# Softmax rows copied to fp32r-typed tiles ahead of three quarters of the last layer's transposes

## The chip, the cores and the metric

One core of a Trainium2 chip runs the whole program. Its engines work side by side, each through its own queue: TensorE (PE, with its weight loads shown apart as PEld), VectorE (DVE), ScalarE (ACT), GpSimd (POOL) and SyncE (SP), which here issues the DMAs. The metric is the device time of one execution, in microseconds; before the change the median of three runs is 1212.86 us (1212.85 to 1212.88).

## The reference

Three layers in sequence, on 8 sequences of 576 positions, in fp32. First an attention over 32 memory slots (8 heads of 64), then a token and channel MLP with residuals, and last the layer that the change touches, four causal attention experts of which each position uses two:

```python
logits = x @ w_gate                      # top 2 of 4 experts, softmax over the two
for e in range(E):                       # E = 4, Hd = 64
    q, k, v = x @ wq[e], x @ wk[e], x @ wv[e]
    scores = scale * (q @ k.transpose(0, 2, 1))
    scores = np.where(causal, -1000000000.0, scores)
    scores = scores - scores.max(-1, keepdims=True)
    a = np.exp(scores)
    a /= a.sum(-1, keepdims=True) + 1e-09
    ye = a @ v @ wo[e]
    out += mask[..., None] * w * ye      # mask: this expert is one of the position's two
```

## The kernel before, in words

Products that need more than fp32r precision are made of three fp32r products: a number is split into a high part of type fp32r and the rest (`split`, `mm3`, L207). The last layer is the last stage of the program, from about 735 us on; the channel MLP's last two chunks of hidden units are computed inside it as filler, in halves of a sequence (`load_2`, `split_2`, `mm1_2`, `load_p2`, `mm2_2`).

**Units.** A unit `n` is one sequence `b` and one expert `e` (n = 4b + e), 32 in all. Its 576 queries are four blocks of 128 rows and a tail of 64; two units (an even and the odd one after it) share one tail of 128 rows. Block `c` sees 128(c + 1) keys, so the blocks have 128, 256, 384 and 512 columns; a unit's four blocks lie side by side in a tile of 1280 columns (`ab`, one of two by the parity of the unit; offsets `aoff`), the tails in `atl`.

**Steps of a unit.** `scores` (L1314 to L1316): the products into PSUM, a masked minimum on VectorE and the exponential on ScalarE into `a`. `norm` (L1344 to L1359): the factors (softmax sum and gate) on VectorE, and then POOL multiplies the four blocks by them, in the order 0, 1, 2, 3 (L1359); the tail is scaled by ScalarE (L1355). `turn` (L1361): TensorE transposes the scaled rows 128x128 at a time into PSUM, as fp32, with an fp32 identity (L1378), and `split` makes high and low parts of them. Block 2 is turned first (3 transposes, and in even units one more of the tail's last columns, L1380), then blocks 0 and 1 together (3), and later block 3 (4) and the tail (`tail_turn`, L1398, 4). `weigh` (L1423) multiplies the transposed rows with the values, and `project` (L1452) makes the output of a sequence from its four experts and stores it.

**The order.** The loop over `t` traces unit `t`'s scores and `norm` and unit `t - 1`'s `turn` and `weigh`, and between them pieces of a list of filler (`some()`). The order in which each engine runs its instructions is then written by the framework, which plays the traced instructions through a simulated timeline (`schedule_with_timeline_sim=True`, with transposes at high priority); the order is fixed in the program, and each engine's queue, SP's too, runs it in order and waits where an operand isn't there.

**Tiles and slots.** A tile name has as many slots as `bufs` says; a new tile of a name waits until all readers of the one that held its slot are done. `u2` (a half's input to the channel MLP, 576 KB) has two slots in the pool `c2`; `p2[1]` borrows one of them. `yb` (a partial sum in `weigh`) has two. The output blocks `osb` have two, from the pool `late` in the last sequence (after `c2` is closed), and there the very last block has two tiles of its own, `oh0` and `oh1`.

Of the kernel before, what the change touches and what calls it, by code (L numbers as in the profile page):

```python
# [9 lines left out]
F32 = mybir.dt.float32  # L10
# [15 lines left out]
def f(ap):  # L26
    return ap.bitcast(F32)
# [140 lines left out]
def fused_kernel(ctx: ExitStack, tc, q, k, v, phi, w_tok1, w_tok2, w_ch1, w_ch2,  # L168
# [695 lines left out]

    c2 = None
    c2_ctx, w3_ctx = ExitStack(), ExitStack()
    u2, uh2, ul2, h2, p2 = {}, {}, {}, {}, {}

    def load_2(j):
        u2[j] = c2.tile([128, KD, SH], F32, name="u2", bufs=2)  # L870
        SP.dma_start(u2[j][:], u_d[:, SH * j:SH * j + SH].rearrange("(c p) s -> p c s", p=128))

    def load_p2(j):
        p2[j] = c2.tile([128, KD, SH], F32, name="u2", bufs=2) if j == 1 else c2.tile([128, KD, SH], F32, name="p2")
        SP.dma_start(p2[j][:], x_d[:, SH * j:SH * j + SH].rearrange("(c p) s -> p c s", p=128))
# [22 lines left out]
    with ExitStack() as sb:  # L898
# [189 lines left out]
        for i in range(NW + LAG):  # L1088
            items = [()] if i == NW else [work[i]] if work[i][0] in WIDE else [(*work[i], 0), (*work[i], 1)]
            for it in items:  # L1090
                if it:
# [10 lines left out]
                    for fc in fcs:  # L1102
# [10 lines left out]
                        if n > WIDE[-1]:  # L1113
                            for _ in range(7):
                                if next(wcl, 0) == 0 and c2 is None:
                                    stg_ctx.close()
                                    c2 = c2_ctx.enter_context(tc.tile_pool(name="c2", bufs=1, side="right"))
                                    load_2(0)
                                    load_2(1)
# [46 lines left out]
    with ExitStack() as sc:  # L1166
# [22 lines left out]
        aoff = [0, 128, 384, 768]  # L1189
        ab = [wk_.tile([128, 1280], F32, name=f"a{i}") for i in range(2)]  # L1190

        atl = wk_.tile([128, 640], F32, name="atl")
# [151 lines left out]
        def norm(n):  # L1344

            b, e = divmod(n, E)
            w = NQ - e % 2
            cf = wk_.tile([128, NQ], F32, name="cf", bufs=2)
            DVE.tensor_scalar_add(cf[:, 0:w], smb[n % 2][:, 0:w], 1e-9)
            DVE.reciprocal(cf[:, 0:w], cf[:, 0:w])  # L1350
            DVE.tensor_mul(cf[:, 0:w], cf[:, 0:w], gt[b][:, e, 0:w])  # L1351
            a = ab[n % 2]
            for c in range(w):
                if c == NQ - 1:
                    ACT.activation(atl[:, 0:S], atl[:, 0:S], AF.Copy, scale=cf[:, c:c + 1])  # L1355
                    continue
                W = 128 * c + 128
                x_ = a[:, aoff[c]:aoff[c] + W]
                POOL.tensor_mul(x_, x_, cf[:, c:c + 1].to_broadcast([128, W]))  # L1359

        def turn(n, c):  # L1361

            e = n % 2
            a = ab[e]
            if n not in aA:
# [10 lines left out]
            with tc.high_priority():  # L1376
                for kc in range(k):
                    PE.transpose(p[:, 128 * kc:128 * kc + 128], a[:, o + 128 * kc:o + 128 * kc + 128], ident[:])  # L1378
                if c == 2 and e == 0:
# [12 lines left out]
        def tail_turn(n):  # L1392
# [3 lines left out]
            with tc.high_priority():  # L1396
                for kc in range(4):
                    PE.transpose(p[:, 128 * kc:128 * kc + 128], atl[:, 128 * kc:128 * kc + 128], ident[:])  # L1398
            split(Bh[:, :, :, 256:320].rearrange("p e k q -> p k e q"), Bl[:, :, :, 256:320].rearrange("p e k q -> p k e q"),
                  p[:].rearrange("p (k e q) -> p k e q", k=4, e=2))  # L1400

        def weigh(n, part):
# [19 lines left out]
            for i, (kc, lo, x) in enumerate(ops):  # L1422
                PE.matmul(p[:, lo:w], lhsT=v_[:, kc, 0, :], rhs=x, start=(i == 0), stop=(i == len(ops) - 1))  # L1423
            t_ = wk_.tile([128, 320], F32, name="yb", bufs=2)
            ACT.activation(t_[0:64, 0:w], p[64:128, 0:w], AF.Copy)
# [26 lines left out]
        def project(b, c):  # L1452
# [3 lines left out]
            cs = slice(0, 128) if last else slice(128 * c, 128 * c + 128)  # L1456
            if b == B - 1 and c == 1:
                for i, w in enumerate((slice(0, 256), slice(256, 512))):
                    p = pp.tile([128, 512], F32, name="g", bufs=GB)[:, 0:256]
                    mm3(p, [((y[0][:, cs], y[1][:, cs]), (woh[:, pr, w], wol[:, pr, w]))  # L1460
                            for pr in range(2) for y in [yT[b, pr][1:]]], late="l")
                    o_ = late.tile([128, 256], F32, name=f"oh{i}")
                    if i:
                        DVE.tensor_copy(o_[:], p)
                    else:
                        ACT.activation(o_[:], p, AF.Copy)
                    SP.dma_start(out[b, cs, w], o_[:])
                return
            p = pp.tile([128, 512], F32, name="g", bufs=GB)
            mm3(p[:], [((y[0][:, cs], y[1][:, cs]), (woh[:, pr, :], wol[:, pr, :]))  # L1470
                       for pr in range(2) for y in [yE[b // 2, pr] if last else yT[b, pr][1:]]], late="l")
            o_ = late.tile([128, 512], F32, name="osb", bufs=2) if late else wk_.tile([128, 512], F32, name="osb", bufs=2)
            if b == B - 1 and c in (3, 0):
# [22 lines left out]
        load_2(2)  # L1496
        load_2(3)
        proj(0, 1, 1, 0, True)
# [4 lines left out]
        for t in range(NE + 2):  # L1503
# [12 lines left out]
            if e == 0:  # L1516
# [6 lines left out]
                if b == B:  # L1523
                    held = [(project, B - 2, c) for c in range(4)]
            elif e == 1:
                if b < B:
                    fill = [(proj, b, 1, i, hf) for i, hf in KQ[2:4]]
                if 0 < b < B - 1 and b - 1 not in HELD:
# [5 lines left out]
            elif e == 2:  # L1534
# [9 lines left out]
                if b + 2 < B:  # L1544
                    fill += [(load_2, 2 * b + 4), (load_2, 2 * b + 5)]
            elif e == 3 and not more:
# [104 lines left out]
```

## Time and profile before

| | |
|---|---|
| median of three runs | 1212.86 us |
| the profiled execution | 1214.76 us |
| its span, first to last instruction | 1213.0 us |
| PE busy | 1165.3 us, 96% |
| PEld busy | 1064.7 us, 88% |
| VectorE busy | 816.3 us, 67% |
| ScalarE busy | 610.8 us, 50% |
| POOL busy | 449.5 us, 37% |
| mean granted clock of TensorE | 0.988 |

The page gives each engine's busy time, the same in 40 equal slices of 30.3 us (a digit is tenths, 9 means 90% or more), the DMA queues, the chain of work that ended last, and groups of equal instructions. The views asked of the trace are a table of busy time by stretches, lists of instructions in order of time, groups by form, the waits and the DMA issues. Matmuls are pipelined: one's duration is longer than the distance to the next.

### The profile page before, as it was taken

The page shows a single profiled execution, that of the slowest core. Times are in us where ns is not written, and L with a number is a line of the kernel's source. Part 1 is how long each engine was busy: PE and PEld are TensorE (multiplying, and loading weights), DVE is VectorE, ACT ScalarE, POOL GpSimd, SP SyncE. Part 2 cuts the span into 40 slices and gives each one's busy share as a digit, 9 for nine tenths or more (in the row PEclk, how much of TensorE's full clock was granted, in tenths as well). Part 3 has the DMA queues.
Part 4 walks back from the last instruction along what each step waited for, and adds up shares of the span by engine and source line. Part 5 has one row for each costly group of instructions (what it writes and reads, how often), then busy time and mean ns, then how long its engine had stood idle before and what let it go on. Part 6 is the DMA issues. An engine that isn't in the chain of part 4 may idle for free.

```text
span 1213.0 us, 23508 instructions
## 1 busy us (share of the span) xinstructions
PE 1165.3 (96%) x8586; PEld 1064.7 (88%) x8586; DVE 816.3 (67%) x1992; ACT 610.8 (50%) x1591; POOL 449.5 (37%) x603
## 2 busy tenths in 40 slices
PE   4899998999999999999999999999999999999998
PEld 3678887999888888889999889999999999999986
DVE  6999998665483756567566514777676767676664
ACT  3565565454442323223322213677676767677775
POOL 2774453442002012112111344545454627383331
PEclk9799999999999999999999999999999999999999
DMA  8896767532370221232123343322333333322522
GB/s 239 251 276 209 215 212 221 171 118 92 97 251 20 105 70 35 71 104 97 43 71 105 96 113 114 88 84 79 84 88 83 102 97 99 94 80 54 166 86 105
DMA packets 133780, 145.07 MB, mean 120 GB/s; under 512 B 35616, under 2 KB 101408, under 8 KB 133664
## 3 DMA queue, kind: packets, MB, share of 16 engines
q1 hardware_dynamic: 133664, 143.57, 39.2%
q8 instruction: 68, 1.11, 0.4%
q14 instruction: 48, 0.39, 0.1%
HBM read 91.10 MB, written 40.89 MB: 109 GB/s over the span
## 4 chain that ended last, share of the span: by engine, by line
PE 79%; DVE 11%; DMA 3%; issue 2%; ACT 2%; POOL 1%; SPq 0%; DVEq 0%; ACTq 0%; POOLq 0%
PE g L207 21%; PE o L207 16%; PE h L207 16%; PE y L1423 4%; PE b L207 3%; PE s L1314 3%; PE b L679 3%; PE t L1378 3%; PE s L1336 1%; DVE ul L670 1%; DVE cy L772 1%; PE g L623 1%; PE g L383 1%; PE g L624 1%; PE g L626 1%
## 5 line engine op out<-in xcount | busy, mean ns | idle before, releaser
L1359 POOL TENSOR_TENSOR a<-a,cf 128x128 f32<-128x128 f32 (+3 forms) x128 | 88.3, 723 | 68.9 <-DVE cf L1351 64.9
L207 PE MATMUL o<-hl,w2h 128*128 128x512 f32 x288 | 112.7, 391 | 0.3 <-DVE hl L931 0.3
L207 PE MATMUL o<-hh,w2l 128*128 128x512 f32 x288 | 112.3, 390 | 0.0
L207 PE MATMUL o<-hh,w2h 128*128 128x512 f32 x288 | 108.7, 392 | 0.2 <-DVE pb L1026 0.2
L930 ACT ACTIVATE hh<-m 128x256 fp32r<-128x256 f32 x96 | 38.9, 416 | 111.8 <-DVE m L1001 72.2
L1303 DVE CUSTOM_DVE_ANT_0 ssb<-s,cmask 128x128 f32<-128x128 f32 (+2 forms) x144 | 68.5, 483 | 27.3 <-PE s L1314 20.5
L1316 ACT ACTIVATE a<-ssb,nb 128x128 f32<-128x128 f32 (+3 forms) x128 | 71.3, 558 | 18.4 <-DVE nb L1303 15.1
L207 PE MATMUL h<-uh,w1h 128*128 128x512 f32 (+2 forms) x200 | 66.5, 334 | 4.7 <-ACT uh L211 4.7
L931 DVE SCALAR_TENSOR_TENSOR hl<-m,hh 128x256 fp32r<-128x256 f32 x96 | 58.2, 615 | 17.6 <-ACT hh L930 15.4
L978 POOL TENSOR_TENSOR tl<-ub,th 128x512 fp32r<-128x512 f32 x12 | 18.1, 1526 | 136.3 <-ACT th L977 136.3
L207 PE MATMUL h<-uh,w1l 128*128 128x512 f32 (+2 forms) x200 | 66.7, 334 | 0.0
L1215 POOL TENSOR_TENSOR xl<-p,xh 128x288 fp32r<-128x288 f32 x60 | 47.4, 811 | 51.8 <-ACT xh L1214 51.6
L207 PE MATMUL h<-ul,w1h 128*128 128x512 f32 (+2 forms) x200 | 66.1, 335 | 0.0
L207 PE MATMUL g<-xh,qkh 128*128 128x288 f32 x232 | 65.3, 301 | 0.0
L207 PEld LDWEIGHTS o<-hh,w2l 128*128 128x128 f32 x288 | 54.1, 188 | 11.3
L207 PE MATMUL g<-xh,qkl 128*128 128x288 f32 x232 | 63.9, 296 | 0.0
L207 PEld LDWEIGHTS o<-hh,w2h 128*128 128x128 f32 x288 | 54.0, 188 | 10.7 <-DVE pb L1026 1.0
L963 POOL TENSOR_TENSOR ub<-ub 128x512 f32<-128x512 f32 x6 | 9.8, 1628 | 144.4 <-DVE ul L214 144.4
L207 PEld LDWEIGHTS o<-hl,w2h 128*128 128x128 f32 x288 | 54.1, 188 | 10.0 <-DVE hl L931 0.6
L214 DVE TENSOR_TENSOR Bl<-t,Bh 128x512 fp32r<-128x512 f32 (+1 forms) x80 | 50.5, 633 | 14.3 <-ACT Bh L211 12.6
L923 DVE SCALAR_TENSOR_TENSOR hl<-h,hh 128x512 fp32r<-128x512 f32 x24 | 16.5, 689 | 59.9 <-ACT hh L922 59.8
L1430 POOL TENSOR_TENSOR yl<-yt,yh 128x256 fp32r<-128x256 f32 x30 | 22.2, 739 | 85.0 <-ACT yh L1429 74.9
(340 smaller groups left out, 4123.8 us busy)
## 6 DMA issues: line engine op xcount, KB each, us to landing
cst<-in_moe_w_ch_dram SPq DMA_DIRECT2D x24, 512.0 KB, 4.8
u_d<-u SPq DMA_DIRECT2D x32, 288.0 KB, 3.6
p_d<-u SPq DMA_DIRECT2D x16, 576.0 KB, 4.2
ub<-u_d SPq DMA_DIRECT2D x9, 1024.0 KB, 5.7
pb<-p_d SPq DMA_DIRECT2D x36, 256.0 KB, 4.1
x_d<-pb SPq DMA_DIRECT2D x36, 256.0 KB, 2.1
u<-u_d SPq DMA_DIRECT2D x16, 576.0 KB, 4.2
p<-x_d SPq DMA_DIRECT2D x15, 576.0 KB, 4.1
```

Of the source, the lines that this page charges most:

```text
L207: PE.matmul(ps, lhsT=a, rhs=b, start=start and i == 0, stop=stop and i == len(seq) - 1)
L214: DVE.tensor_sub(lo, src, f(hi))
L679: PE.matmul(h1[j, fc, "p"][:], lhsT=w[:, kd, :], rhs=x[:, kd, :], start=(part == 0 and i == 0), stop=(part == 1 and i == KD - 1))
L930: ACT.activation(hh, c, AF.Relu)
L931: DVE.scalar_tensor_tensor(hl, c, 0.0, f(hh), op0=OP.max, op1=OP.subtract)
L1215: POOL.tensor_sub(xl[b][:, c, ss], x_, f(xh[b][:, c, ss]))
L1303: DVE.tensor_tensor_reduce(out=out, in0=p, in1=mask, scale=-scale, scalar=least, op0=OP.add, op1=OP.min, accum_out=acc)
L1314: PE.matmul(p[:, 0:W], lhsT=q_[n][:, 128 * c:128 * c + 128], rhs=kk[n][:, 0:W], start=(i == 0), stop=(i == 1))
L1316: ACT.activation(a[:, aoff[c]:aoff[c] + W], s_[:, 0:W], AF.Exp, scale=-1.0, bias=nb[:, 0:1], accum_out=sm[:, c:c + 1])
L1359: POOL.tensor_mul(x_, x_, cf[:, c:c + 1].to_broadcast([128, W]))
L1378: PE.transpose(p[:, 128 * kc:128 * kc + 128], a[:, o + 128 * kc:o + 128 * kc + 128], ident[:])
L1423: PE.matmul(p[:, lo:w], lhsT=v_[:, kc, 0, :], rhs=x, start=(i == 0), stop=(i == len(ops) - 1))
```

## The change

For units 0 to 30, `norm` copies the scaled blocks 0 and 1 (one DMA), the scaled block 3 (another), and for even units the first 512 columns of the scaled tail (a third), as raw bits, from the fp32 tiles to tiles of type fp32r (`ar`, 1280 columns, and `atr`, 512, one slot each). The transposes of these read the copies with an fp32r identity and write PSUM through an fp32r view. Block 2 of every unit, the last unit's blocks, and the tail's last columns are transposed from the fp32 tiles as before. The order of scaling becomes block 2, then 0 and 1, then 3, and the tail's ScalarE product is traced ahead of them.

To make room in SBUF, `u2` gets one slot in `c2` and, for the half j = 1 alone, one in a pool of its own, and the loads of odd halves are traced a unit or more later; `yb` gets one slot; `osb` always comes from the stage's pool, and the last output block takes one of its two slots in place of `oh0` and `oh1`.

```diff
-        u2[j] = c2.tile([128, KD, SH], F32, name="u2", bufs=2)
+        u2[j] = (wk8 if j == 1 else c2).tile([128, KD, SH], F32, name="u2")
...
-        p2[j] = c2.tile([128, KD, SH], F32, name="u2", bufs=2) if j == 1 else c2.tile([128, KD, SH], F32, name="p2")
+        p2[j] = c2.tile([128, KD, SH], F32, name="u2" if j == 1 else "p2")
...
+        identr = wk_.tile([128, 128], F32R, name="identr")
+        ACT.activation(identr[:], ident[:], AF.Copy)
...
-            for c in range(w):
-                if c == NQ - 1:
-                    ACT.activation(atl[:, 0:S], atl[:, 0:S], AF.Copy, scale=cf[:, c:c + 1])
-                    continue
-                W = 128 * c + 128
-                x_ = a[:, aoff[c]:aoff[c] + W]
-                POOL.tensor_mul(x_, x_, cf[:, c:c + 1].to_broadcast([128, W]))
+            copied = n < NE - 1
+            ar[n] = wk_.tile([128, 1280], F32R, name="ar") if copied else a
+            if e % 2 == 0:
+                ar["t"] = wk_.tile([128, 512], F32R, name="atr")
+                ACT.activation(atl[:, 0:S], atl[:, 0:S], AF.Copy, scale=cf[:, NQ - 1:NQ])
+            for cs in ((2,), (0, 1), (3,)):
+                for c in cs:
+                    W = 128 * c + 128
+                    x_ = a[:, aoff[c]:aoff[c] + W]
+                    POOL.tensor_mul(x_, x_, cf[:, c:c + 1].to_broadcast([128, W]))
+                if copied and cs != (2,):
+                    o = slice(aoff[cs[0]], aoff[cs[-1]] + 128 * cs[-1] + 128)
+                    SP.dma_start(f(ar[n][:, o]), a[:, o])
+                if e % 2 == 0 and cs == (2,):
+                    SP.dma_start(f(ar["t"][:, 0:512]), atl[:, 0:512])
...
-            a = ab[e]
+            a, idn, ty = (ar[n], identr, F32R) if n < NE - 1 and c != 2 else (ab[e], ident, F32)
...
-                    PE.transpose(p[:, 128 * kc:128 * kc + 128], a[:, o + 128 * kc:o + 128 * kc + 128], ident[:])
+                    PE.transpose(p[:, 128 * kc:128 * kc + 128].bitcast(ty), a[:, o + 128 * kc:o + 128 * kc + 128], idn[:])
...
-                    PE.transpose(p[:, 128 * kc:128 * kc + 128], atl[:, 128 * kc:128 * kc + 128], ident[:])
+                    PE.transpose(p[:, 128 * kc:128 * kc + 128].bitcast(F32R), ar["t"][:, 128 * kc:128 * kc + 128], identr[:])
...
-            t_ = wk_.tile([128, 320], F32, name="yb", bufs=2)
+            t_ = wk_.tile([128, 320], F32, name="yb")
...
+                o2 = wk_.tile([128, 512], F32, name="osb", bufs=2)
...
-                    o_ = late.tile([128, 256], F32, name=f"oh{i}")
+                    o_ = o2[:, w]
...
-            o_ = late.tile([128, 512], F32, name="osb", bufs=2) if late else wk_.tile([128, 512], F32, name="osb", bufs=2)
+            o_ = wk_.tile([128, 512], F32, name="osb", bufs=2)
...
-        load_2(3)
...
+                if more:
+                    fill += [(load_2, 2 * b + 3)]
...
-                    fill += [(load_2, 2 * b + 4), (load_2, 2 * b + 5)]
+                    fill += [(load_2, 2 * b + 4)]
```

## Rows read from the trace of the kernel before

**Rows 1.** The page, busy shares of the span and busy tenths in 40 slices

```profile
PE 1165.3 (96%) x8586; PEld 1064.7 (88%) x8586; DVE 816.3 (67%) x1992; ACT 610.8 (50%) x1591; POOL 449.5 (37%) x603
...
PE   4899998999999999999999999999999999999998
```

**Rows 2.** Table by stretches of the last layer; the first row names its columns

```profile
core 0: us, PE busy (x) PEld busy (x) DVE busy (x) ACT busy (x) POOL busy (x), PEclk, DMA share, GB/s
776.00:1160.00 384.00, 379.85 (x2840) 370.13 (x2840) 272.62 (x877) 277.45 (x809) 196.69 (x302) 1.00 0.32 89
1160.00:1213.00 53.00, 46.96 (x271) 40.09 (x269) 25.99 (x80) 33.08 (x83) 14.19 (x22) 0.98 0.32 109
```

**Rows 3.** PE's longest wait from 735 us on: total, times, longest

```profile
PE s L1314 <- DMA qa<-qb: 2.1, 1, 2.1
```

**Rows 4.** Products by form: count, busy us, mean ns of one, idle before

```profile
L1378 PE MATMUL t<-ident,a 128*128 128x128 f32 x320 | 48.8, 274 | 0.1
...
L207 PE MATMUL h<-th,sh 128*128 128x256 f32 x144 | 40.7, 282 | 0.0
...
L1398 PE MATMUL t<-ident,atl 128*128 128x128 f32 x64 | 10.0, 275 | 0.2 <-DVE Bt L1390 0.2
...
L1423 PE MATMUL y<-Al,vhl 128*128 128x128 f32 x24 | 5.3, 223 | 0.0
...
L1380 PE MATMUL t<-ident,atl 128*128 128x128 f32 x16 | 4.4, 272 | 0.0
```

**Rows 5.** PE in order of time at 1025 us: start, us, instruction, count

```profile
1025.75 0.82 PE L1378 MATMUL t<-ident,a 128*128 128x128 f32 x6
1026.40 0.27 PE L1380 MATMUL t<-ident,atl 128*128 128x128 f32 x1
```

**Rows 6.** Weight loads of ordinary fp32r products by form, 128 and 64 columns

```profile
L207 PEld LDWEIGHTS g<-vgh,xh 128*128 128x128 f32 x128 | 24.2, 189 | 0.6 <-ACT kk L1235 0.4
...
L207 PEld LDWEIGHTS g<-vgh,xh 128*64 128x64 f32 x32 | 4.3, 134 | 0.0
```

**Rows 7.** Loads of fp32 transposes (L521, L525) and an fp32 product: min/median/max ns

```profile
L525 PEld LDWEIGHTS t<-ident,at x16: 108/110/128, 35.7 to 305.7; 128*64 128x64 f32 x16
...
L521 PEld LDWEIGHTS t<-ident,at x64: 137/141/229, 31.7 to 304.9; 128*128 128x128 f32 x64
...
L393 PEld LDWEIGHTS g<-ones,es x28: 186/190/338, 38.5 to 272.3; 128*128 128x128 f32 x28
```

**Rows 8.** DMA issues: count, KB each, median us from issue to landing

```profile
u<-u_d SPq DMA_DIRECT2D x16, 576.0 KB, 4.2
...
qb<-qa SPq DMA_DIRECT2D x32, 144.0 KB, 2.4
...
y_d<-yl SPq DMA_DIRECT2D x6, 256.0 KB, 2.6
...
out_dram<-osb SPq DMA_DIRECT2D x8, 128.0 KB, 2.4
...
out_dram<-oh SPq DMA_DIRECT2D x2, 128.0 KB, 2.2
```

**Rows 9.** Scaling and transposes in order of time, first and third batch

```profile
776.95 2.76 POOL L1359 TENSOR_TENSOR a<-a,cf 128x128 f32<-128x128 f32 x4 [0.73 <-DVE cf L1351]
...
779.16 0.82 PE L1378 MATMUL t<-ident,a 128*128 128x128 f32 x6
...
885.77 5.47 POOL L1359 TENSOR_TENSOR a<-a,cf 128x128 f32<-128x128 f32 x8 [7.59 <-DVE cf L1351]
...
892.45 0.62 PE L1378 MATMUL t<-ident,a 128*128 128x128 f32 x4
```

**Rows 10.** SP's queue in order of time, loads of `u2`

```profile
737.41 0.39 SPq L871 DMA_DIRECT2D u<-u_d  x1
...
751.50 1.12 SPq L871 DMA_DIRECT2D u<-u_d  x2
```

**Rows 11.** SP's queue at the end, the last stores

```profile
1208.08 0.59 SPq L1479 DMA_DIRECT2D out_dram<-osb  x1
...
1209.39 0.89 SPq L1467 DMA_DIRECT2D out_dram<-oh  x2
```

More of the change, by code (lines that the diff above doesn't have):

```diff
@@ L862, in fused_kernel @@
         stg_ctx.close()
-    c2 = None
+    c2 = wk8 = None
     c2_ctx, w3_ctx = ExitStack(), ExitStack()
@@ L1116, in fused_kernel @@
                                     stg_ctx.close()
+                                    wk8 = sb.enter_context(tc.tile_pool(name="wk8", bufs=1))
                                     c2 = c2_ctx.enter_context(tc.tile_pool(name="c2", bufs=1, side="right"))
@@ L1190, in fused_kernel @@
         ab = [wk_.tile([128, 1280], F32, name=f"a{i}") for i in range(2)]
+        identr = wk_.tile([128, 128], F32R, name="identr")
+        ACT.activation(identr[:], ident[:], AF.Copy)
+        ar = {}
         atl = wk_.tile([128, 640], F32, name="atl")
@@ L1461, in project @@
                             for pr in range(2) for y in [yT[b, pr][1:]]], late="l")
-                    o_ = late.tile([128, 256], F32, name=f"oh{i}")
+                    o_ = o2[:, w]
                     if i:
-                        DVE.tensor_copy(o_[:], p)
+                        DVE.tensor_copy(o_, p)
                     else:
-                        ACT.activation(o_[:], p, AF.Copy)
-                    SP.dma_start(out[b, cs, w], o_[:])
+                        ACT.activation(o_, p, AF.Copy)
+                    SP.dma_start(out[b, cs, w], o_)
                 return
@@ L1525, in fused_kernel @@
             elif e == 1:
+                if more:
+                    fill += [(load_2, 2 * b + 3)]
                 if b < B:
-                    fill = [(proj, b, 1, i, hf) for i, hf in KQ[2:4]]
+                    fill += [(proj, b, 1, i, hf) for i, hf in KQ[2:4]]
                 if 0 < b < B - 1 and b - 1 not in HELD:
```

## The prediction

> **What bounds the kernel now.** I read the page's busy shares and slices first: TensorE (PE) is busy 96% of the span, and in the last 14 of 40 slices, where the changed stage lies, PE stands at 9 in all but the last one [rows 1]. The table by stretches says the same in microseconds: from 776 to 1160 us PE is busy 379.85 of 384 us at a granted clock of 1.00 (the level of 2.4 GHz), and the next engines, ScalarE and VectorE, only some 72% of it; in the last 53 us, the last batch, PE is idle for 6 us [rows 2]. The list of waits names no wait of PE above 2.1 us in the whole stage [rows 3]. So from 776 to 1160 us a nanosecond taken out of PE is a nanosecond of time, as long as what PE does next is ready; in the last batch it is not, because there a chain of latencies sets the end.
>
> **The transposes, the term that decides.** The stage makes 320 + 64 + 16 = 400 transposes of 128x128 [rows 4]. The change turns to the new type: for units 0 to 30 the 3 of the first two row blocks and the 4 of the fourth, 31 x 7 = 217, and all 64 of the tails (16 unit pairs x 4); 281 together. The 96 of the third block, the 7 of unit 31 and the 16 of `atl`'s last columns stay as they are.
> Cost of one now: six start at 1025.75 and the next at 1026.40, so 0.65/6 = 108 ns apart [rows 5]. A product takes as long as the slower of its two halves, the load of its 128 columns and the streaming. Streaming: a transpose lasts 274 ns; fp32r products of 128 and 256 columns last 223 and 282 ns, that is 59 ns for 128 columns on a fixed part of 164 [rows 4]. So the fp32 transpose streams 274 - 164 = 110 ns, its own pitch, and an fp32r one should stream about 59. Loading: in ordinary products 64 columns take 134 ns and 128 take 189 [rows 6], 55 ns for 64 more, so 110 for 128; in transposes 64 take 110 and 128 take 141 [rows 7], 31 ns for 64 more, so 62 for 128. It is the operation and not the type that makes the short load: the one ordinary fp32 load of 128 columns takes 190 [rows 7]. So if the fp32r transpose keeps the transposing load, its pitch is the larger of 59 and 62, about 60 ns, and one transpose saves 48 ns. No row shows an fp32r transpose. The ends are 0 saved (it loads as the ordinary fp32r product does, at 110) and 49 saved (streaming alone); a loss on PE itself I exclude, since neither half is slower than 110 ns in any of these rows. I take 48 because the loads of 141 ns are the nearest rows: same operation, same width.
> There is a rule that speaks against it. The Trainium skill ("TensorE: Matmul & The Clock Gate", section "LDWEIGHTS (loading the stationary operand)") says that a weight load takes its columns divided by 1.2, whatever the rest; for 128 columns this is an estimate of 107 ns, just the pitch of now, and the transposes would be no faster in any type. The ordinary loads agree (55 ns for 64 columns more), the transposing ones do not (31 ns) [rows 6, 7]; that is why I give it a rival of its own and not the forecast.
> On the path: 29 of the 281 (units 28 to 30: 21, and the last two tails: 8) lie in the last batch, where PE has slack; I count them nothing. The other 252 x 48 ns = **12.1 us** saved.
>
> **The copies.** Each of units 0 to 30 gets two copies (196 and 256 KB) and each even unit a third (256 KB): 62 + 16 = 78 DMAs in SP's queue. The trace has on-chip copies of 144 KB at 2.4 us from issue to landing and a 256 KB transfer out of SBUF at 2.6 [rows 8], some 0.5 to 0.6 us of SP's time for an issue [rows 11]. 78 x 0.55 = 43 us of issues are a small part of SP's time in a stage of 430 us, and nothing computes there. What counts is whether a copy has landed when its turn comes. The first unit of a batch is tight: at the latest of eight, scaling starts at 776.95 and the group with its third, second and first block's transposes at 779.16, 2.2 us later [rows 9]. With the third block scaled first, the first two are done 0.73 + 0.40 + 0.57 = 1.70 us after the start (the four products of a unit take 2.76 us) and landed some 4.2 us after it (0.1 to the issue, 2.4 transfer), at 781.1; the three transposes were due 0.33 us after the group's first, 779.5: 1.6 us late. The same subtraction gives 1.2 us in the third batch and at most 0.3 in each of the other six. In all some 3.6 us. SP issues its swaps and stores in the same stretch, so a copy can stand two issues longer, 1.1 us x 8 batches. Bounds: 0 (PE does other work meanwhile; the order of PE's work is planned with the copies in it) to 3.6 + 8.8 = 12.4 us. I take **2 us**, near the lower end, because each batch's first unit falls where other products are ready.
> The scaling itself only changes order; for the last unit the fourth block, which it turns first, is still scaled last. The single `ar` buffer makes a unit's copies wait for the transposes of the unit before; that is priced as a rival (C). The tail's ScalarE product and `yb` with one buffer (VectorE reads it right behind ScalarE) I put at nothing: VectorE's addition follows the ScalarE copy at once and the next use is a product group later; without that cover one addition, under 0.5 us, would show.
>
> **The loads.** `u2` falls from two slots to one. In the steady state a half is loaded in 4.2 us [rows 8] as soon as the one before is split, long before its use: nothing. Once, at the start, it shows: the second batch's first half was loaded at 737.41; now its slot is held by `p2[1]`, until 751.50, when the trace's next load takes the slot that `p2[1]` leaves [rows 10]. It lands near 755.7 instead of 741.6, and the 24 products on it (2 chunks x 12, of 288 columns) come later. At 59 ns for 128 columns, 0.133 us each, 3.2 us is the upper end, 0 the lower; other products are ready there (projections, values), so I take **0.5 us**.
>
> **The end.** The last output block used two buffers of its own. Now it takes an `osb` slot, the one that the fifth block (its last store issued at 1208.08 [rows 11]) holds until that has landed, 2.4 us later [rows 8], 1210.5. Its copies out of PSUM then end near 1210.9, its two stores go at about 1211.0 and 1211.4 and land 2.2 us later [rows 8]; before, the two were issued between 1209.39 and 1210.28 [rows 11], the second at about 1209.9. **+1.5 us**, with 0 as the lower end if the slot is free.
>
> **Sum**: -12.1 + 2.0 + 0.5 + 1.5 = -8.1 us. The profiled execution took 1214.76 us (span 1213.0); the median of the runs is 1212.86, 1.90 less, and 8.1 us off either leaves the same difference: **1204.8 us** for the median.
>
> **Rivals.**
> A. *The transposes are no faster*, because the new type is loaded at 110 ns for 128 columns like all fp32r products. For it: every fp32r load in the trace is of that kind. Against: the short load of the transposes. Then only the costs stay: 1212.9 + 2.0 + 0.5 + 1.5 = **1216.9**. Chance 0.20.
> B. *The copies are late at the first unit of each batch*: faster transposes, but the upper half of the bound, 8 us instead of 2: **1210.8**, or 1208 to 1212. For it: lateness of up to 1.6 us above and SP's full queue. Against: the ready work of other kinds. Chance 0.13.
> C. *The slower side: SP's queue is held by the copies.* They wait in order for the unit before to finish its transposes (one `ar`): in the third batch eight products run from 885.77 on, so unit 1's first two blocks are scaled by 890.2, but unit 0's fourth block is turned until 893.07 [rows 9], 3 us in which whatever stands behind them in SP's queue waits: swaps of `qa` and `qb`, the `qz` copies, stores, and through the swaps the scores of the next unit; the largest wait of PE in the stage is already of that kind, 2.1 us [rows 3]. Priced at 2.5 us of PE idle in each of 7 batches, 17.5 us: 1204.8 + 17.5 - 2.0 = **1220.3**. It turns the sign from 1.4 us a batch on (10.1/7). Against it: swaps stand at other times in most batches. Chance 0.10.
>
> **Numbers.** Forecast 0.57, with its own range 1200 to 1209. Within 0.2% (2.4 us, about what a measurement of this kernel can tell from no change) needs a time from 1210.4 to 1215.3: the lower half of A's costs and the upper part of B, 0.11. Faster by more: the forecast and half of B, 0.64. Slower by more: most of A, and C, 0.25. The range 1199 to 1217 leaves out C and the last of A.
>
> **What would show it.** The transposes of the first, second and fourth blocks and of the tail would start 55 to 65 ns apart, with loads of about 140 ns; a pitch near 110, or loads near 190, is rival A and makes the prediction wrong. The stretches of the stage would shorten by about 1.7 us a batch (36 x 48 ns) with PE still over 98% busy. Waits of PE for a DMA into `ar` should sum to under 3 us; 8 us is B, and waits of scores for the swaps C. The last chain should show the last output copy behind a store from `osb`.

## The result, and the profile after

The changed kernel takes 1222.28 us (median of 4 runs, 1219.39 to 1224.68) against 1212.87 us of the kernel before on the same chip: a ratio of 1.0074 with a 95% interval of 1.0062 to 1.0086. It is 0.74%, 9 us, **slower**, where 8 us faster was predicted. The profiled execution took 1222.56 us, its span is 1220.7 us, the mean granted clock 0.992.

Rows of the page of the changed kernel (line numbers from L1114 on differ from before): busy time, PE's tenths in 40 slices, and the chain of work that ended last; the fourth row is the same chain before.

```profile
PE 1164.2 (95%) x8586; PEld 1059.2 (87%) x8586; DVE 819.2 (67%) x1992; ACT 610.1 (50%) x1592; POOL 450.5 (37%) x603
...
PE   5889998999899999999999999999999999999987
...
PE 76%; DVE 13%; DMA 4%; ACT 3%; issue 2%; POOL 1%; SPq 1%; DVEq 0%; ACTq 0%; POOLq 0%
...
PE 79%; DVE 11%; DMA 3%; issue 2%; ACT 2%; POOL 1%; SPq 0%; DVEq 0%; ACTq 0%; POOLq 0%
```

PE has hardly less busy time than before (1165.3, [rows 1]), and it stands in more places: the last two slices went from 9, 8 to 8, 7, and the chain runs through PE for 76% instead of 79% of the span.

The table of busy time by stretches (stretch and its length, then PE, PEld, DVE, ACT, POOL with their instructions, PE's granted clock, DMA share, GB/s). The first row is of the kernel before, the other three are of the changed kernel:

```profile
735.00:776.00 41.00, 40.16 (x303) 39.33 (x303) 23.52 (x77) 18.95 (x63) 19.33 (x31) 1.00 0.45 125
...
735.00:776.00 41.00, 38.28 (x286) 37.12 (x284) 22.37 (x78) 19.96 (x65) 16.61 (x28) 1.00 0.35 94
776.00:1160.00 384.00, 378.55 (x2845) 366.10 (x2844) 273.25 (x865) 274.51 (x799) 198.10 (x304) 1.00 0.44 135
1160.00:1221.00 61.00, 50.00 (x280) 42.35 (x278) 28.25 (x90) 34.98 (x89) 14.17 (x22) 0.95 0.36 126
```

The middle stretch holds 2845 products where it held 2840 [rows 2]: as many in the same time, although 36 transposes of each batch are now the shorter kind. The last stretch takes 61 us instead of 53, with 11 us of PE idle instead of 6. In the first stretch of the stage PE works 38.28 us; before it was 40.16.

The transposes, by form: duration min/median/max in ns, then first and last start (L1391 is `turn`, L1411 the tail; `ar`, `atr` are the copies, `a` the fp32 rows).

```profile
L1391 PEld LDWEIGHTS t<-identr,ar x217: 137/140/145, 782.7 to 1194.8; 128*128 128x128 f32 x109
L1391 PE MATMUL t<-identr,ar x217: 219/245/282, 782.8 to 1194.8; 128*128 128x128 f32 x109
...
L1391 PE MATMUL t<-ident,a x103: 270/272/328, 780.5 to 1203.9; 128*128 128x128 f32 x103
...
L1411 PEld LDWEIGHTS t<-identr,atr x64: 137/139/145, 786.7 to 1197.0; 128*128 128x128 f32 x64
L1411 PE MATMUL t<-identr,atr x64: 222/247/252, 786.7 to 1197.1; 128*128 128x128 f32 x64
```

All 281 are there, their loads keep the short 140 ns, and the product is some 27 ns shorter than the fp32 one. How that looks in order of time, PE and then its loads, beside [rows 5]:

```profile
1012.33 0.37 PE L1391 MATMUL t<-identr,ar 128*128 128x128 f32 x3
1012.54 0.46 PE L1319 MATMUL s<-kk,qa 128*128 128x512 f32 x1
1012.84 0.39 PE L1319 MATMUL s<-kk,qb 128*128 128x512 f32 x1
...
1012.20 0.36 PEld L1391 LDWEIGHTS t<-identr,ar 128*128 128x128 f32 x3
1012.50 0.19 PEld L1319 LDWEIGHTS s<-kk,qa 128*128 128x128 f32 x1
```

One by one, the three products start 63 and 64 ns apart and the scores product 80 behind the last; the loads of the second and the third start 85 ns apart, and the scores' load another 85 behind. In the 28 groups of four of `ar` the medians are 59, 65, 85 and 86 ns from product to product, some 75 in the mean. The loads set the larger of these. This is seen where the product before had ended when a group began, so that nothing else was in the way of its loads (start, length of all; fp32 in the kernel before, two loads, and fp32r in the changed kernel, four):

```profile
1085.59 0.20 PEld L1398 LDWEIGHTS t<-ident,atl 128*128 128x128 f32 x2 [0.31 <-PE y L1423]
...
1071.67 0.39 PEld L1411 LDWEIGHTS t<-identr,atr 128*128 128x128 f32 x4 [0.19 <-PE s L1319]
```

A load lasts 0.14 us, so the two fp32 loads start 0.06 us apart and the fp32r ones 0.083. In the last layer of the changed kernel no load starts sooner than 82 ns after the load of an fp32r transpose (281 of them, median 85); before, 21 of 400 start 57 to 65 ns after that of an fp32 one, and most of the others 109 ns after it, the pace of the products.

The scores product behind the group, whose load could start only at 1012.50, lasts 0.46 us in place of 0.39: part of the gain is handed on to the next load. From the start of such a group to where the product behind it is through its own pitch, four transposes took 0.440 us as fp32 and 0.366 as fp32r (medians of 47 groups before and 44 after), **19 ns** less for each, not 48.

PE's waits from 735 us on, changed kernel (total, times, longest), beside [rows 3]:

```profile
PE s L1341 <- DMA qz<-qb: 2.3, 1, 2.3
PE t L207 <- DVE kk L1241: 2.0, 2, 1.6
PE t L1391 <- DVE Bl L214: 1.8, 2, 1.0
PE t L1391 <- DMA ar<-a: 1.5, 1, 1.5
...
PE s L1341 <- DMA qz<-qa: 1.2, 2, 0.8
```

Waits for a copy are small (1.5 us). The largest is for a transfer of the tail's queries (`qz`), and it lies in the last batch. There SP's queue runs like this (changed kernel, SP in order of time; last row the last stores):

```profile
1168.16 0.48 SPq L1330 DMA_DIRECT2D qz<-qb  x1
1168.69 0.59 SPq L1372 DMA_DIRECT2D atr<-atl  x1
1169.38 1.20 SPq L1370 DMA_DIRECT2D ar<-a  x2
...
1173.04 1.27 SPq L1330 DMA_DIRECT2D qz<-qa  x2
1174.47 1.12 SPq L1370 DMA_DIRECT2D ar<-a  x2
1175.64 0.59 SPq L1495 DMA_DIRECT2D out_dram<-osb  x1
1176.28 0.46 SPq L1330 DMA_DIRECT2D qz<-qb  x1
...
1217.68 0.81 SPq L1481 DMA_DIRECT2D out_dram<-osb  x2
```

Two copies and a store stand ahead of the last `qz<-qb`. The chain of work that ended last goes through it (start, us, piece):

```profile
1166.97 2.38 DMA qa<-qb
...
1173.78 0.22 PE t L1391 x3
...
1176.28 3.79 DMA qz<-qb
1180.11 0.53 PE s L1341 x2
```

Before, the chain of the same batch ran through products and scalings without a DMA, up to its last stores. The `qz<-qb` is not only issued late: it lands 3.79 us after its issue, where the median of its 32 is 1.8, and 1.80 in experiment 4, in which no copy goes ahead of it. And what held SP's queue in the stage from 776 us on (total, times, longest):

```profile
SPq L1370 <- PE t L1391: 51.9, 18, 4.9
```

That is the copies of a unit, at the head of the queue, waiting for the transposes of the unit before to leave the one `ar` slot: rival C's mechanism, 51.9 us in 18 waits. The sum alone says little: before, the loads of `u2` held the same queue in the same stage for as long, waiting for `u2`'s slots:

```profile
SPq L871 <- POOL ul L885: 56.1, 10, 11.5
```

To say where the time went I use one measure for all kernels. The **stage** is the time from the first product of the channel MLP's second half (L207, `g`) to the last product of the program. **PE's need** is the sum over all products in it of the distance between two of that form when nothing holds them (0.1085 us for an fp32 transpose, 0.075 for an fp32r one, 0.1325 for 288 columns, 0.232 for 512, and so on from the traces; it is good to about 1.5 us: for the five kernels below whose products are the same, before, 1, 2, 5 and 12, it comes out between 451.5 and 454.7). The rest is PE standing, in short holds that the busy share doesn't show as well as in idle time. The last batch is counted from the third-block transposes of unit 28.

| kernel | stage us | PE's need | PE standing | of the stage: last batch |
|---|---|---|---|---|
| before | 473.8 | 453.1 | 20.7 | 40.0 |
| after | 481.0 | 444.3 | 36.7 | 45.7 |

PE needs 8.8 us less, as 281 times 33.5 ns makes 9.4, and the stage takes 7.2 us more. So in these terms there are 16 us of new standing: 5.7 + 1 in the last batch (need there 36.7 and 35.7), the others before it. 2.8 of the 16 are the loads' doing: at their pace of 85 ns in place of 75 the 281 transposes need that much more, and some 13 us are left.

### The profile page after: what moved, and what is told of

Same layout as the page of the kernel before. It is cut to its first block, busy times and chain, and to the rows that moved or that the text cites. A ratio compares the mean times of both kernels' runs of the same rounds, so it can differ in the third digit from the quotient of the medians.

```text
span 1220.7 us, 23647 instructions
## 1 busy us (share of the span) xinstructions
PE 1164.2 (95%) x8586; PEld 1059.2 (87%) x8586; DVE 819.2 (67%) x1992; ACT 610.1 (50%) x1592; POOL 450.5 (37%) x603
## 4 chain that ended last, share of the span: by engine, by line
PE 76%; DVE 13%; DMA 4%; ACT 3%; issue 2%; POOL 1%; SPq 1%; DVEq 0%; ACTq 0%; POOLq 0%
PE g L207 21%; PE o L207 15%; PE h L207 15%; PE y L1436 4%; PE b L207 4%; PE b L679 3%; PE s L1319 3%; PE t L1391 2%; DVE ul L670 2%; PE s L1341 1%; DVE cy L772 1%; DMA ub<-u_d 1%; PE g L623 1%; PE g L626 1%; PE g L624 1%
## 5 line engine op out<-in xcount | busy, mean ns | idle before, releaser
L1367 POOL TENSOR_TENSOR a<-a,cf 128x256 f32<-128x256 f32 (+3 forms) x128 | 88.1, 721 | 78.1 <-DVE cf L1356 72.8
L207 PE MATMUL o<-hl,w2h 128*128 128x512 f32 x288 | 112.8, 392 | 0.3 <-DVE hl L931 0.3
L207 PE MATMUL o<-hh,w2l 128*128 128x512 f32 x288 | 112.4, 390 | 0.0
L207 PE MATMUL o<-hh,w2h 128*128 128x512 f32 x288 | 108.8, 393 | 0.7 <-DVE pb L1026 0.7
L207 PE MATMUL h<-uh,w1h 128*128 128x512 f32 (+2 forms) x200 | 66.9, 336 | 5.1 <-ACT uh L211 5.1
L207 PE MATMUL h<-uh,w1l 128*128 128x512 f32 (+2 forms) x200 | 66.7, 334 | 0.0
L207 PE MATMUL h<-ul,w1h 128*128 128x512 f32 (+2 forms) x200 | 65.8, 334 | 0.0
L207 PE MATMUL g<-xh,qkh 128*128 128x288 f32 x232 | 65.0, 302 | 0.0
L207 PEld LDWEIGHTS o<-hh,w2l 128*128 128x128 f32 x288 | 54.1, 188 | 11.4
L207 PEld LDWEIGHTS o<-hh,w2h 128*128 128x128 f32 x288 | 54.0, 188 | 11.4 <-DVE pb L1026 1.2
L207 PE MATMUL g<-xh,qkl 128*128 128x288 f32 x232 | 63.7, 296 | 0.0
L207 PEld LDWEIGHTS o<-hl,w2h 128*128 128x128 f32 x288 | 54.1, 188 | 10.2 <-DVE hl L931 0.8
```

Source lines behind the costliest of these rows:

```text
L207: PE.matmul(ps, lhsT=a, rhs=b, start=start and i == 0, stop=stop and i == len(seq) - 1)
```

## The experiments

Ratios are to the kernel before on the same chip, with 95% intervals.

**1. The copies without the faster transposes.** Unit 0 to 30 copied as in the change, and the copies transposed as fp32.

```diff
-            a, idn, ty = (ar[n], identr, F32R) if n < NE - 1 and c != 2 else (ab[e], ident, F32)
+            a, idn, ty = (f(ar[n][:]), ident, F32) if n < NE - 1 and c != 2 else (ab[e], ident, F32)
...
```

> The changed kernel with all its copies, slots and order of scaling, but the copies are transposed as fp32 with the fp32 identity (the copies read through an fp32 view). Theory Q (the loss is in SP's queue and in the slots; the fp32r transposes themselves save some 18 ns each, 281 of them, because a group's first load and the load behind it still take the long pitch): 1222.3 + 5 = 1227, 1224 to 1230. Rival P (the fp32r transposes save their full 33 ns of pitch): 1222.3 + 9 = 1231. Rival N (nothing is saved on TensorE): 1222, unchanged.

Measured: 1225.28 us, 1.0115 [1.0099, 1.0130]. The changed kernel is at 1.0074, so on top of everything else the fp32r transposes are worth 0.41%, 5.0 us or 18 ns each, close to the 19 of a group. They do pay; what surrounds them costs 1.15%, 14 us. (The two orders of work differ as well; see experiments 10 to 12 for what that can do.)

**2. The memory alone.** The kernel before with `u2`'s slots and later loads, one `yb`, the last block in `osb`; no copies.

```diff
-        u2[j] = c2.tile([128, KD, SH], F32, name="u2", bufs=2)
+        u2[j] = (wk8 if j == 1 else c2).tile([128, KD, SH], F32, name="u2")
...
-            t_ = wk_.tile([128, 320], F32, name="yb", bufs=2)
+            t_ = wk_.tile([128, 320], F32, name="yb")
...
-                    o_ = late.tile([128, 256], F32, name=f"oh{i}")
+                    o_ = o2[:, w]
```

> The kernel before with the slots alone: u2 with one slot and its later loads, yb with one, osb for the last block; no copies, fp32 transposes, old order of scaling. Theory Q: the late first load costs 2.5 us and the last block's slot 1 us: 1212.9 + 3.5 = 1216.4, 1215 to 1218. Rival M (the slots, not the copies, make the loss): 1220 to 1223. Rival that they cost nothing: 1213.

Measured: 1217.10 us, 1.0049 [1.0036, 1.0062]. Making room costs 6 us by itself, two thirds of the whole loss. The step from here to experiment 1 (1.0115), the copies and the new order of scaling, is 0.66%, 8 us.

**3. The transposes without copies or memory.** The kernel before; the same 281 transposes as fp32r, on rows that ScalarE and POOL write as fp32r in place. The rows' low parts are thereby left out of the result.

```diff
-        ab = [wk_.tile([128, 1280], F32, name=f"a{i}") for i in range(2)]
+        ab = [wk_.tile([128, 1280], F32R, name=f"a{i}") for i in range(2)]
...
```

> The kernel before with the same 281 transposes as fp32r but without any copy: ScalarE and POOL write the softmax rows as fp32r in place, so their low parts are left out (rounded away). Slots and order of scaling as before. Theory Q: 252 transposes on the path x 18 ns: 1212.9 - 4.5 = 1208.4, 1207 to 1210. Rival P: 252 x 33 ns = 8.3, 1204.6. Rival N: 1213.

Measured: 1208.37 us, 0.9980 [0.9970, 0.9990]. It is 2.5 us faster than before. Its PE needs 445.0 us, 8.1 less, and its stage takes 470.2, only 3.6 less: even with no copy in the way, less than half of that reaches the end. By the 19 ns of a group 281 transposes would be worth 5.3 us.

**4. The last batch without copies.** The change, but units 28 to 31 transposed as fp32 without copies.

```diff
-            copied = n < NE - 1
+            copied = n < NE - E
...
```

> The changed kernel, but the last batch's four units are transposed from the fp32 tiles as before and not copied. Theory Q: in the last batch TensorE stood 10.2 us idle against 3.4, behind qz and qa copies that SP issued late; without the softmax copies in its queue some 6 us come back: 1216, 1214.5 to 1218. Rival: the last batch's loss comes from the slots or from the new order of work, then 1221 to 1223.

Measured: 1217.62 us, 1.0057 [1.0044, 1.0070]. The last batch falls from 45.7 to 41.2 us, and in its waits no DMA is left. Of these 4.5 us the profiled execution keeps 3.6 in its stage (477.4), the times 0.17%, 2 us, with intervals that overlap. The trace shows that the copies cost time there; the times alone do not, and they are not the bulk.

**5. `u2` alone.** The kernel before with `u2`'s edit of experiment 2 and nothing else.

```diff
-        u2[j] = c2.tile([128, KD, SH], F32, name="u2", bufs=2)
+        u2[j] = (wk8 if j == 1 else c2).tile([128, KD, SH], F32, name="u2")
...
-        load_2(3)
...
```

> The kernel before with u2's single slot and its later loads alone (two osb tiles and yb as before). The slots together cost 0.49%, 6.0 us. Theory L (the load of the second batch's first half, held by p2[1]'s slot, makes the most of that): 4.5 to 5 us, 0.37 to 0.41%, about 1215.6 where before is 1211; the trace should show the delay in the stage's first 50 us. Rival (the loss is osb's and yb's): under 2 us, 1213 or less.

Measured: 1218.01 us, 1.0039 [1.0025, 1.0053]. The largest single piece: 0.39%, 4.7 us; its stage is 3.9 us longer. Nearly all of this is there after the first 60 us of the stage (before, and this run):

```profile
734.31:794.31 60.00, 59.16 (x445) 57.99 (x444) 38.89 (x127) 33.56 (x103) 35.97 (x56) 1.00 0.43 121
...
734.08:794.08 60.00, 56.84 (x417) 54.46 (x416) 36.35 (x121) 31.94 (x95) 33.58 (x53) 1.00 0.37 102
```

PE has run 28 products fewer by then, some 3.6 us of its work. The load of the second batch's first half goes out at 750.78 us in place of 737.41 [rows 10], and the first unit's tail columns are transposed 5.0 us later from the stage's start on. No single wait of PE there is above 0.6 us.

**6. The copies issued by POOL.** The change with its three copies taken out of SP's queue.

```diff
-                    SP.dma_start(f(ar[n][:, o]), a[:, o])
+                    POOL.dma_start(f(ar[n][:, o]), a[:, o])
...
```

> The changed kernel, but its 78 copies are issued by POOL, which has just made the data, in place of SP. Theory S (copies in SP's queue wait there for the one ar slot, 52 us in 18 waits, and hold swaps and qz copies behind them): SP is as free as before, the last batch's 5 us come back, ratio 1.0074 to about 1.0035, 1215 where before is 1211. Rival (the wait moves to POOL and holds scaling and splits there, and a copy issued by POOL costs its time): 1220 or more.

Measured: 1255.59 us, 1.0347 [1.0332, 1.0362]. The wait for the slot moves to POOL (first row, POOL's waits) and there, behind it, stand the scaling and the splits; PE's waits for VectorE's additions to `p` come to 15.7 us (second row, PE's waits of the same kernel), where the change's longest of any kind is 2.3.

```profile
POOL ar L1370 <- PE t L1391: 16.9, 7, 3.9
...
PE g L207 <- DVE p L1218: 15.7, 6, 6.3
```

It rules out the simple cure. As it also puts the issues themselves on POOL, it does not say what SP's queue alone costs: an issue takes 0.54 to 0.58 us of POOL's own time, some 42 us for the 78.

**7. Two tiles in place of `ar`.** Blocks 0 and 1 get a tile with two slots, block 3 one of its own.

```diff
-            ar[n] = wk_.tile([128, 1280], F32R, name="ar") if copied else a
+            ar[n, 0] = wk_.tile([128, 384], F32R, name="arl", bufs=2) if copied else None
+            ar[n, 3] = wk_.tile([128, 512], F32R, name="arh", bufs=1) if copied else None
...
```

> The changed kernel with ar as two tiles: blocks 0 and 1 in one of 384 columns with two slots, block 3 in one of 512 with one. Theory S: the first copy of a unit never waits for the unit before, the second only for that unit's last transposes; SP's waits for transposes fall from 52 us to under 25 and 2 to 4 us come back, 1216 to 1218 where before is 1211. Rival (the hold in SP's queue costs nothing, the copies cost by their landing time alone): 1220, unchanged.

Measured: 1218.84 us, 1.0046 [1.0033, 1.0060], 0.28% or 3.4 us better than the change. The wait that held SP's queue for 51.9 us is now (SP's waits)

```profile
SPq L1371 <- PE t L1392: 18.6, 11, 2.9
...
SPq L1371 <- POOL a L1368: 16.4, 24, 2.6
```

and the wait for `qz<-qb` is no longer among those of PE of 0.9 us or more. The copies now stand 16.4 us in the queue for their scaling, which in the change was 3.1, so in all the copies hold the queue some 20 us less, not 33. This speaks for rival C, but 3.4 us is also what a new order of work can make by itself (experiments 10 to 12).

**8. The last output block in `osb` alone.** The kernel before with that edit of experiment 2.

```diff
-                    o_ = late.tile([128, 256], F32, name=f"oh{i}")
+                    o_ = o2[:, w]
...
```

> The kernel before with the last output block in an osb slot, and osb always from the stage's pool; nothing else. Theory: the last store waits for one slot, 1.1 us by the trace (last product to end of span 6.1 us against 4.9), 0.09%: 1212.1 where before is 1211. Rival: nothing, since the slot is free by then; or over 2 us, if the stage's osb slots also hold the last batch's other blocks.

Measured: 1214.64 us, 1.0008 [0.9999, 1.0017]. PE runs its products here in the very order of before. Its last stores (SP in order of time; in the second fence the kernel before)

```profile
1208.14 0.61 SPq L1482 DMA_DIRECT2D out_dram<-osb  x1
...
1210.48 0.81 SPq L1468 DMA_DIRECT2D out_dram<-osb  x2
```

```profile
1208.76 0.54 SPq L1481 DMA_DIRECT2D out_dram<-osb  x1
```

go out 2.34 us after the `osb` store ahead of them. Before, from that store to the first of `oh` at 1209.39 [rows 11], it was 0.63. From the start of the last product to the end of the span it is 6.1 us in place of 4.8. So the end costs 1 us by the times and 1.3 by the trace, with an interval of the times that reaches zero.

**9. `p2[1]` in the slot of `p2`.** The change, with the first load of `u2` no longer behind `p2[1]`.

```diff
-        p2[j] = c2.tile([128, KD, SH], F32, name="u2" if j == 1 else "p2")
+        p2[j] = c2.tile([128, KD, SH], F32, name="p2")
```

> The changed kernel, but p2[1] takes the slot of p2 in place of u2's, so u2's one slot is free for the second batch's first half from the start. Theory L (u2's 0.39% is that one late load): most of 4.7 us come back, ratio 1.0074 to 1.004, and the stage's first unit is turned some 2 us earlier. Since the changed kernel's own first unit is only 1.6 us late (5.0 with the slots alone), the rival is that a later part of the plan pays: then 1.006 or more.

Measured: 1221.23 us, 1.0075 [1.0063, 1.0087]: nothing. The load goes out at 721.40 us and the first unit's tail columns are transposed 0.3 us late instead of 1.6, but the stage is 481.2 us all the same. The edit does not take the late load away, though, it moves it: `p2[1]` now waits for `p2[0]`'s slot, its load goes out at 740.04 us where in the change it went at 722.29, and PE's longest wait in the first 60 us is the one for the additions to it (SP in order of time, then PE's waits):

```profile
740.04 0.37 SPq L875 DMA_DIRECT2D p<-x_d  x1
...
PE g L207 <- DVE p L1218: 2.3, 2, 1.7
```

In the change that kind of wait is 0.6 us there, and the longest is 1.6 (`kk`). So this run does not say what the late first load costs.

**10. Experiments 4, 7 and 9 together.**

```diff
-            copied = n < NE - 1
+            copied = n < NE - E
...
-        p2[j] = c2.tile([128, KD, SH], F32, name="u2" if j == 1 else "p2")
+        p2[j] = c2.tile([128, KD, SH], F32, name="p2")
...
+            ar[n, 0] = wk_.tile([128, 384], F32R, name="arl", bufs=2) if copied else None
+            ar[n, 3] = wk_.tile([128, 512], F32R, name="arh") if copied else None
...
```

> The changed kernel with three repairs together: ar as two tiles (two slots and one), no copies in the last batch, p2[1] in its own slot. If the costs add (3.4 + 2.4 + 3 to 4.7 us of 9.0), it ends at 1.0000 to 0.9990 of the time before, the fp32r transposes' 4.9 us less the last store's 1 us and what the copies still cost. Rival (the repairs overlap, since each shifts the same work): 1.002 to 1.004, still slower than before.

Measured: 1219.40 us, 1.0062 [1.0045, 1.0079]. The repairs don't add up: together they give 0.12%, less than experiment 7 alone, with an interval that overlaps those of both 7 and the change. Each edit makes the framework write another order; that such orders differ by microseconds of themselves is the reading that is left, and no row shows it.

**11. and 12. Only what fits.** The kernel before with copies of block 3 alone (31 of 78 copies, 124 transposes), both slots of `u2`, `osb` and `oh` as they were, `yb` with one slot; scaling in the old order. In 11 the copies are transposed as fp32r, in 12 as fp32.

```diff
+                if c == 3 and n < NE - 1:
+                    ar[n] = wk_.tile([128, 512], F32R, name="arh")
+                    SP.dma_start(f(ar[n][:]), x_)
...
-            a = ab[e]
+            a, idn, ty = (ar[n], identr, F32R) if n < NE - 1 and c == 3 else (ab[e], ident, F32)
...
```

> The kernel before with copies and fp32r transposes of the fourth block alone (31 copies, 124 transposes), both slots of u2, the block's copy in a slot of its own (512 columns), osb and oh as before; only yb goes to one slot. If the loss of the changed kernel is u2's slot plus the copies of the first two blocks and tails (the ones that are needed soonest), this wins what 124 transposes are worth: by the group cost of the traces, 0.111 less 0.092 us each, about 2.3 us, ratio 0.997 to 0.999. If any copy through SP's queue costs its share of the changed kernel's 0.66% for 78 copies, 31 of them cost 0.26%, 3.2 us, and the ratio is 1.000 to 1.002. My first prediction's 48 ns a transpose would give 6 us, 0.995.

> The same 31 copies of the fourth block, but transposed as fp32 from the copy, so that copies are there and no transpose is faster. Against the kernel with the fp32r transposes of these copies it shows what 124 transposes are worth (2.3 us, 0.2%, by the group cost; 6 us, 0.5%, by the prediction); against the kernel before, what 31 copies cost without u2's change: 1.000 to 1.001 if a copy that is needed late is free, 1.0026 if each copy costs its share of the 78.

Measured: 11 takes 1210.50 us, 0.9972 [0.9961, 0.9984], **faster than before by 0.28%, 3.4 us**; 12 takes 1218.03 us, 1.0037 [1.0027, 1.0048]. The table of stretches of 11:

```profile
735.00:776.00 41.00, 40.41 (x309) 40.09 (x309) 23.49 (x81) 20.94 (x67) 20.24 (x33) 1.00 0.46 121
776.00:1160.00 384.00, 381.17 (x2859) 371.45 (x2858) 277.31 (x888) 279.00 (x815) 196.52 (x304) 1.00 0.37 109
1160.00:1209.00 49.00, 41.41 (x240) 35.19 (x238) 22.76 (x64) 29.18 (x71) 12.22 (x19) 0.97 0.38 128
```

Its copied transposes by form:

```profile
L1385 PEld LDWEIGHTS t<-identr,arh x124: 137/140/146, 781.0 to 1184.4; 128*128 128x128 f32 x124
L1385 PE MATMUL t<-identr,arh x124: 222/245/256, 781.0 to 1184.5; 128*128 128x128 f32 x124
```

PE's longest wait in it, and the wait of the copies in SP's queue:

```profile
PE t L1385 <- DVE Bl L214: 1.8, 2, 1.6
...
SPq L1366 <- PE t L1385: 46.2, 14, 6.0
```

The same fp32r form as in the change (245 ns, loads 140). In the middle stretch 2859 products find room where 2840 did [rows 2], and PE waits for no copy. SP's queue is held for 46.2 us by its copies, nearly as long as in the change, and here no wait of PE comes of it: by this a held queue is dear only where something that is due stands behind it.

The same measure as above for the kernels that matter:

| kernel | stage us | PE's need | PE standing | of the stage: last batch |
|---|---|---|---|---|
| 1, copies as fp32 | 486.1 | 453.7 | 32.4 | 44.3 |
| 2, memory alone | 478.4 | 451.5 | 26.9 | 40.1 |
| 3, no copies | 470.2 | 445.0 | 25.2 | 40.9 |
| 4, last batch fp32 | 477.4 | 443.3 | 34.1 | 41.2 |
| 5, `u2` alone | 477.7 | 454.3 | 23.4 | 40.2 |
| 7, two tiles | 478.3 | 446.8 | 31.5 | 40.1 |
| 11, block 3 alone | 470.3 | 449.8 | 20.5 | 40.9 |
| 12, the same as fp32 | 477.5 | 454.7 | 22.8 | 41.7 |

In 11 PE needs 3.3 us less and the stage takes 3.5 us less. PE stands as long as before. This is the one kernel in which the shorter pitch reaches the end whole, as far as a measure that is good to 1.5 us can tell.

11 and 12 differ in nothing but the type, and their times by 0.65%, 8 us, which is 64 ns for each of 124 transposes and more than any of them can save. By the traces, 11 is ahead by 3.0 us when unit 24's third block comes, after 96 copied transposes, 31 ns each, where a group gives 19; the other 4 us arise in the last two batches, where the two orders differ most and the 28 copied transposes left can save 0.9 us. So at least 3 us of the difference come with the order and not with the type, and 12's 0.37% is no clean price of 31 copies. By the same measure the 3.4 us that 11 is ahead of before are no clean price of 124 transposes either; by the group they are worth 2.4.

## Why the prediction was wrong

**The transposes: right kind, wrong size.** "If the fp32r transpose keeps the transposing load, its pitch is the larger of 59 and 62": the load keeps its length (140 ns) and not its pace, and this is the step that failed. I read the pace off the lengths (31 ns for 64 columns more, so 62 for 128) and held that "it is the operation and not the type that makes the short load". For fp32 transposes 62 is right (loads as little as 57 ns apart), but behind an fp32r one the next load starts no sooner than 82 ns later, 85 in the median. Rival A, 110 ns, is out, and half of its reason stands: the type does count. The streaming of 59 ns is hidden behind these loads, and no row speaks against it. The second thing that I left out is the ordinary load behind each group, which the shorter last transpose no longer covers. With both, a transpose in a group of four saves 19 ns and not 48. The term of -12.1 us is -4.8 by the group (252 times 19 ns), and on the chip it was -5.0 (the change against experiment 1) or -2.5 (experiment 3). The Trainium skill ("TensorE: Matmul & The Clock Gate", section "LDWEIGHTS (loading the stationary operand)") has a load take its columns divided by 1.2, an estimate of 107 ns for 128. Ordinary loads agree (the two of the scores behind the group shown start at 1012.50 and 1012.61); those of the transposes, 57 and 82 ns apart at the least, do not, and the measurement decides.

**The loads: +0.5 predicted, 4.7 measured** (experiment 5). The place was right and the size failed. I priced one late load at the start, between 0 and 3.2 us, and took 0.5 because other products would be ready. In experiment 5 PE is some 3.6 us of work behind after the first 60 us, of 3.9 in the whole stage: the late half was not covered. Experiment 9 does not speak against this, since it makes another load late instead. With one slot each later load also goes out later: the last load of `u2` was issued at 1037.01 us before, at 1080.23 in the change, at 1074.20 in experiment 5. The loads land 4.2 us after issue as before. "In the steady state ... long before its use: nothing" may hold; no run shows a cost there. The changed kernel is 22 products behind after its first 60 us, but copies fall into the same stretch, so how much of the 4.7 us it pays is not shown either.

**The copies: +2 predicted, 8 measured** (experiments 1 and 2). Where I looked, at the first unit of each batch, little was lost: waits for `ar` are 1.5 us, and the copies land about as priced, 2.2 us (192 KB, not 196) and 2.5 us (256 KB) after their issue. What I had made rival C, with a chance of 0.10 and a price of 17.5 us, is seen in its place: copies in SP's in-order queue wait for the one slot and hold what stands behind. In the last batch, which I had left out of C, it is plain: a 2.3 us wait for `qz<-qb` behind two copies and a store, on the chain that ended last. Experiments 4 and 7 give back 2 and 3.4 us, and 1.5 together with 9 (experiment 10), so how much of the 8 is C's is not shown. I counted that batch as having slack; its slack is that of PE, and the chain of transfers, scores and transposes has none.

**The end: +1.5 predicted, about 1 measured** (experiment 8). Right, as far as an interval that reaches zero can say. `yb`'s one slot, put at nothing, has no run of its own; experiments 5 and 8 add up to 0.47% of experiment 2's 0.49%, so it is small.

**The sum.** Measured by ratios: memory +0.49%, copies and new order +0.66%, transposes -0.41%, together +0.74%; in us +6, +8, -5 against +2.0 (loads and end), +2.0 and -12.1. All three of the terms were wrong in the same direction, the gain most. That each is measured as a difference of two kernels, with an order of work of its own in each, may leave some 3 us of doubt in any one of them. The time, 1222.28, lies beyond the range, whose upper end left out C though C's own 1220.3 was the nearest of all cases.

**What stays open.** Which holds make up the standing in the body of the change (up to unit 24's third block: need 358.1 us in place of 367.8, some 2.5 of the difference being products that fall behind the cut; time 383.4 in place of 383.0). The order is written anew for each kernel, and in experiments 10 and 12 some 3 to 4 us seem to go with such orders. No run separates the copies from the new order of scaling, or has all 78 copies with both slots of `u2`, for which the change had to make room.

## What to carry to other kernels

A faster instruction is worth what its group takes from entry to exit, the delayed load behind it included, not the difference of two pitches; and it is worth that only if nothing else has to move for it. The length of an instruction in a trace is not its pace: two loads of 140 ns followed each other here after 57 or after 82 ns, by the type. Price the room that a change takes (slots, later loads) and the queue that it uses as terms of their own, by one run each: here the room (0.49%) cost as much as the instruction gave (0.41%). Then keep the part that needs neither: copies of the last-scaled block alone, for which no other tile gave up room but `yb`, made the kernel 0.28% faster, where all of them made it 0.74% slower.

## What the runs showed of the hardware that was not expected

- The load of an fp32r transpose of 128x128 is as long as that of an fp32 one (140 ns), and the next load starts no sooner than 82 ns after it (median 85 of 281), where it can start 57 ns after an fp32 transpose's. The fp32 transposes run 109 ns apart all the same, the fp32r ones up to 86.
- The same copies issued from POOL's queue in place of SP's cost 2.7% of the whole kernel (1.0347 against 1.0074); the issues take some 42 us of POOL's own time (0.54 to 0.58 each) and the waits in front of its work 16.9 us, and what each costs was not taken apart.
